# Scores of 64 queries on four quadrants, and longer tiled operations, in attention between two layers' matmuls

## The chip, the cores and the metric

The kernel runs on one core of a Trainium2 chip. Time is the device time of one execution in microseconds. TensorE does all matmuls and transposes, ScalarE, VectorE and GpSimd the elementwise work; SyncE and, for the first loads, GpSimd issue the DMAs.

## What is computed

Attention over 4 batches, 8 heads, 576 positions of 64 elements, then two feed-forward layers on its 2304 x 512 output. From the reference, shortened:

```
scores = where(causal, -1e9, q @ k.T / 8)                 # 576 x 576 of each head
a = exp(scores - max);  a /= a.sum + 1e-9;  local = a @ v
q_p = phi(q);  mem_out = (q_p @ M_prev) / (q_p . z_prev + 1e-6)
x = g * mem_out + (1 - g) * local                         # 2304 tokens x 512
h = x @ w_in;  r = max(h, 0);  x = (s * r * r + b) @ w_out         # first layer, 512 -> 2048 -> 512
h = x @ w2_in; g = piecewise quadratic of h;  out = g @ w2_out     # second layer
```

## The kernel before

**Units of work.** A head pair (hp) is two heads side by side on 128 partitions, 64 each. The queries of a batch are cut into tiles of 128 (t = 0 to 3) and a last one of 64 (t = 4). A part of attention is one batch and one of two groups: "lo" has tiles 1 and 0 (256 queries), "hi" has tiles 4, 3 and 2 (320 queries). The eight parts, the eight blocks of the first layer and the column sums stand in the program in an order of their own (ORDER); a part has four head pairs, so there are 16 head pairs of each group.

**One head pair.** att_load brings q and k (qk, two buffers) and q, M and v (nv, two buffers). att_front makes phi(q) over its norm and turns it (L796). att_scores writes the scores into PSUM banks ab (four, L826): with 64 elements to contract, each head uses one half of the array's rows, 64x128, and for the 64 queries of tile 4 a quadrant, 64x64, head 0 the first and head 1 the last. VectorE adds the mask and takes the minimum (L837), ScalarE the exponential (L522), and one of three engines scales the rows by the inverse of their sum (L861 to L863) in the arrays aa (four). att_flip turns 128x128 blocks of aa (L881) and copies them into at, au or av. att_sum accumulates the product with M (L896, whole array) and with v (L905, half of the columns for each head) in one bank, and writes the result's rounded and remaining part to xx. All of attention's matmuls are in plain fp32, which takes two records in the trace for each; transposes take one.

**The layers** work in rounded parts (three matmuls of 256 columns for each product: L951 to L953 and L1014, L1015, L1019 in the first layer; L1181 to L1237 and L1213 to L1255 in the second). The last block of the first layer is 512 wide. Their weights are in SBUF; the second layer's replace the first's as the last block is done with them, and its buffers lie where attention's were, so they open when attention has ended.

**What sets the order.** Every operation is given to a planner (Plan) with its engines, cost, dependencies and the slots of pools that it takes. The planner writes one order for each engine; then the program is emitted in it. A scores operation, a flip, a sum are each one entry on TensorE's queue, and nothing stands between their matmuls. While attention runs, layer-1 matmuls of an earlier block fill TensorE's queue between its operations. L1309 are matmuls on zeros that fill waits near the start. The planner gives a group of tiled matmuls the cost c_pair: 0.2 us, 1.667 ns a column and 4 ns a matmul.

Names in the trace: ab the four banks of attention, hb and yb the banks of the layers, wir and wor buffers that the first two parts borrow from weights.

Of the kernel before, what the change touches and what calls it, by code (L numbers as in the profile page):

```python
# [109 lines left out]
class Plan:  # L110
# [26 lines left out]
    def add(self, ways, r=(), w=(), pr=2, acq=()):  # L137
        i = len(self.ops)
        pre = set()
        slots = set(acq)  # L140
        for k in list(r) + list(w):
            s = k[0] if isinstance(k, tuple) else k
            if isinstance(s, Slot):
                slots.add(s)
# [225 lines left out]
def c_pair(n, k=1):  # L370

    return 0.2 + n * 1.667e-3 + k * 0.004
# [3 lines left out]
def tile_kernel(ctx: ExitStack, tc: tile.TileContext, qk_in, nv_in, z_prev, beta,  # L376
# [47 lines left out]
    zr = t32r([P, P], "zr")  # L424
    con = t32([P, 36], "con")
    cs_t = t32([P, NK], "cs")
# [138 lines left out]
    def constants():  # L565
# [6 lines left out]
        for j in range(2):  # L572
            dve(0.08, lambda rows=slice(64 * j, 64 * j + 64), j=j: nc.vector.tensor_scalar(
                con[rows, 32:36], con[rows, 16:24].rearrange("p (n two) -> p n two", two=2)[:, :, j], 1.0, None, ALU.mult), ["con"], ["con"], ATT)
        dma(lambda: con[:, 0:1], lambda: s_in.unsqueeze(0).broadcast_to([P, 1]), 512, w=["sb"], pr=W1)
        dma(lambda: con[:, 1:2], lambda: b_in.unsqueeze(0).broadcast_to([P, 1]), 512, w=["sb"], pr=W1)
# [224 lines left out]

    def att_scores(hp, g, qk, group):

        zs = [R_AB.take() for _ in range(1 + max(x for *_, places in group for x, _ in places))]
        new = []
        for t, c0, c1, _ in group:
            if t == 0:
                att_open[0] = (att_open[1][0], R_SM.take(), 256)  # L810
                new.append(att_open[0][1])
            elif c0 == 0:


                att_open[t] = ([(E_AA if early_part[0] else R_AA).take() for _ in range(1 if t == 4 else 2)], R_SM.take(), 0)
                new += att_open[t][0] + [att_open[t][1]]
# [12 lines left out]
        for t, c0, c1, places in group:  # L829
            w = t * P + rows_of(t)  # L830
            arrays, s, ao = att_open[t]
            nh = len(arrays)
# [3 lines left out]
            for j, (a, (x, at)) in enumerate(zip(arrays, places)):  # L836
                dve(c_dve(c1 - c0) + 0.02, alone(lambda a=a, s=s, z=zs[x], c0=c0, c1=c1, m0=m0, pi=pi, j=j, at=at, ao=ao: nc.vector.tensor_tensor_reduce(  # L837
                    a.t[:, ao + c0:ao + c1], z.t[:, at:at + c1 - c0], mask[:, m0:m0 + c1 - c0], -SCALE,
                    BIG if pi == 0 else s.t[:, j:j + 1], ALU.add, ALU.min, s.t[:, 2 * pi + j:2 * pi + j + 1])),
                    [zs[x], "mask", "zero_aa", (a, "new"), (s, "new")], [(a, t), (s, "min", j)], ATT)  # L840
            if c1 < w:
                continue
            for j, a in enumerate(arrays):
                def view(w=w, a=a, ao=ao):
                    return a.t[:, ao:ao + w]

                act(view, view, AF.Exp, w, [(s, "min", j)], [(a, t), (s, "sum", j)],
                    ATT, ap=2, bias=lambda s=s, x=2 * pi + j: s.t[:, x:x + 1], scale=-1.0,
                    accum_out=lambda s=s, x=4 + j: s.t[:, x:x + 1])
            c = 32 + hp if t == 4 else 16 + 2 * hp  # L850
            dve(0.13, lambda s=s, nh=nh, c=c: nc.vector.scalar_tensor_tensor(
# [3 lines left out]
            for j, a in enumerate(arrays):  # L855
# [3 lines left out]
                def col(s=s, j=j):  # L859
# [3 lines left out]
                     ("ACT", c_act(w, 1), lambda view=view, col=col: nc.scalar.activation(view(), view(), AF.Copy, scale=col()))],  # L863
                    [(s, "i")], [(a, t)], ATT)
        return [t for t, c0, c1, _ in group if c1 == t * P + rows_of(t)]

    def att_flip(t):

        nb = t + 1
        arrays, _, ao = att_open[t]  # L870
        at = R_AT[t].take()
# [3 lines left out]
        for c0, c1 in zip(cuts, cuts[1:]):  # L875
# [6 lines left out]
            pe((c1 - c0) * c_tr(P), flip, [(a, t) for a, kt in blocks[c0:c1] if kt == 0 or t == 4] + ["ident", "zero_aa"], [z, (at, "new", c0)],  # L882
               ATT, [z] + [at] * (c0 == 0))
# [3 lines left out]

    def att_sum(hp, b, g, nv, pg, ats):

        nq = GLEN[g]  # L890
        base = BASE[PARTS.index((b, g))]
        z = R_AB.take()
        keys = [x for t in GROUPS[g] for x in ats[t][1]]

        def go():
            nc.tensor.matmul(z.t[:, 0:nq], nv.t[:, NV_M[g]], pg.t[:, 0:nq], start=True, stop=False)  # L896
            off = 0
            for t in GROUPS[g]:
                n, nb, at = rows_of(t), t + 1, ats[t][0]
                for kt in range(nb):  # L900
                    for j in range(2):
                        last = t == GROUPS[g][-1] and kt == nb - 1
                        own = slice(64 * j, 64 * j + 64)
                        c = kt * P + j * n if t == 4 else (j * nb + kt) * P
                        nc.tensor.matmul(z.t[own, off:off + n], nv.t[:, NV_V[g] + kt, own], at.t[:, c:c + n],  # L905
                                         start=False, stop=last)
                off += n
        cols = nq + sum((t + 1) * rows_of(t) for t in GROUPS[g])
        pe(c_pair(cols, 12), go, [(nv, ""), pg] + keys, [z], ATT, [z])
        cuts = [0] + [c for c in range(nq) if c and (base + c) % XC == 0] + [nq]  # L910
        for a, e in zip(cuts, cuts[1:]):
            c = (base + a) % XC
            xk = x_keys(hp, c, c + e - a)
            rnd(lambda a=a, e=e, c=c: xh[hp][:, c:c + e - a], lambda a=a, e=e: z.t[:, a:e], e - a, [z], ["h" + x for x in xk], ATT, True)
            sub(lambda a=a, e=e, c=c: xl[hp][:, c:c + e - a], lambda a=a, e=e: z.t[:, a:e], lambda a=a, e=e, c=c: xh[hp][:, c:c + e - a],
                e - a, [z] + ["h" + x for x in xk], ["l" + x for x in xk] + [f"early{base}_{hp}"] * early_part[0], ATT, True)

    SCORES = {"lo": [[(1, 0, 256, ((0, 0), (1, 0))), (0, 0, 128, ((0, 256), (1, 256)))]],
              "hi": [[(4, 0, 512, ((0, 0),)), (4, 512, 576, ((1, 384),)), (2, 0, 384, ((1, 0), (2, 0)))],
                     [(3, 0, 512, ((0, 0), (1, 0)))]]}  # L920
    att_open = {}

    def att(i):
# [5 lines left out]
        first = True  # L929
        for hp in range(NP):  # L930
            qk, nv = att_load(b, hp, g, zb)
            if first:
                if "con" not in plan.lw:
                    constants()
                dma(lambda: zb.t, lambda: z_prev[b].rearrange("h d -> (h d)").unsqueeze(0).broadcast_to([P, H * D]),
                    P * H * D * 4, [], [zb], ATT if i == 0 else LOAD, [zb])
                first = False
            pg = att_front(hp, g, nv, zb)
            ats = {}
            for group in SCORES[g]:  # L940
                for t in att_scores(hp, g, qk, group):
                    ats[t] = att_flip(t)
            att_sum(hp, b, g, nv, pg, ats)
        plan.phase = None
# [432 lines left out]
```

## Time and profile before

| | |
|---|---|
| median of 3 runs | 1003.35 us (1003.24 to 1005.19) |
| the profiled execution | 1006.14 us |
| its span, first to last instruction | 1004.4 us |
| TensorE, VectorE, ScalarE, GpSimd busy | 992.5, 660.0, 589.0, 206.3 us |
| mean granted TensorE clock | 0.995 of full speed |

Busy time of an engine is the time in which at least one of its instructions is in flight; a matmul's duration holds its way through the array, so that neighbours overlap, and what one costs in a row is the distance of its start to the next one's.

### The profile page before, as it was taken

Reading aid. Unit: us, or ns where it says so; the run is one execution under the profiler, and the core shown is the slowest. Engines: PE = TensorE matmul, PEld = TensorE weight load, DVE = VectorE, ACT = ScalarE, POOL = GpSimd, SP = SyncE. Lnnn points to the kernel's source line nnn. Section 1 sums busy time; section 2 is a strip of 40 time slices with the busy share of each in tenths; the row PEclk is TensorE's granted clock in tenths of the full one; section 3 lists DMA queues with packets and bytes.
Section 4 is the critical chain, followed back from the end, with each engine's and each line's share of the span. In section 5 each row is a group of like instructions: output and inputs, shape, how many; then the busy total and the mean of one; then the engine's idle time right before and its main releaser. Section 6 shows DMA issues by size and latency. Waiting matters only on the chain.

```text
span 1004.4 us, 19651 instructions
## 1 busy us (share of the span) xinstructions
PE 992.5 (99%) x7480; PEld 878.5 (87%) x7480; DVE 660.0 (66%) x1545; ACT 589.0 (59%) x1331; POOL 206.3 (21%) x320
## 2 busy tenths in 40 slices
PE   8999999999999999999999999999999999999998
PEld 7799998898898889789898888999899998999987
DVE  5899855635644545554687885788769555576742
ACT  5999876646656655565556555666546434254323
POOL 5411133211110211111132321232234101011100
PEclk8999999999999999999999999999999999999999
DMA  9491034211221211211043334634354971231301
GB/s 321 170 410 60 15 92 140 70 52 49 76 70 48 85 62 56 68 60 46 1 152 132 127 116 143 225 126 147 110 185 162 355 248 46 82 95 32 106 27 37
DMA packets 50718, 115.57 MB, mean 115 GB/s; under 512 B 5440, under 2 KB 16192, under 8 KB 50624
## 3 DMA queue, kind: packets, MB, share of 16 engines
q1 hardware_dynamic: 50400, 113.73, 33.2%
q8 instruction: 59, 0.97, 0.4%
q0 software_dynamic: 224, 0.59, 0.3%
q14 instruction: 35, 0.29, 0.1%
HBM read 87.56 MB, written 26.74 MB: 114 GB/s over the span
## 4 chain that ended last, share of the span: by engine, by line
PE 91%; ACT 3%; DVE 2%; DMA 2%; issue 1%; SPq 0%; POOL 0%; DVEq 0%; POOLq 0%; ACTq 0%
PE hb L951 6%; PE hb L953 6%; PE hb L952 6%; PE ab L826 6%; PE yb L1014 5%; PE yb L1019 5%; PE yb L1015 5%; PE ab L905 4%; PE ab L881 4%; PE yb L1213 3%; PE yb L1214 3%; PE yb L1220 3%; PE ab L1220 3%; PE ab L1213 3%; PE ab L1214 3%; PE ab L1182 3%
## 5 line engine op out<-in xcount | busy, mean ns | idle before, releaser
L951 PE MATMUL hb<-xx,wi 128*128 128x256 f32 (+1 forms) x512 | 152.7, 298 | 0.0
L952 PE MATMUL hb<-xx,wi 128*128 128x256 f32 (+1 forms) x512 | 149.5, 292 | 0.0
L953 PE MATMUL hb<-xx,wi 128*128 128x256 f32 (+1 forms) x512 | 149.5, 292 | 0.0
L1014 PE MATMUL yb<-gg,wo 128*128 128x256 f32 (+1 forms) x394 | 102.6, 292 | 1.5 <-ACT gg L537 1.2
L951 PEld LDWEIGHTS hb<-xx,wi 128*128 128x128 f32 x512 | 96.4, 188 | 7.0 <-issue 3.5
L952 PEld LDWEIGHTS hb<-xx,wi 128*128 128x128 f32 x512 | 96.3, 188 | 2.8
L953 PEld LDWEIGHTS hb<-xx,wi 128*128 128x128 f32 x512 | 96.2, 188 | 2.9
L1015 PE MATMUL yb<-gg,wo 128*128 128x256 f32 (+1 forms) x394 | 98.0, 281 | 0.0
L522 ACT ACTIVATE aa<-aa,sm 128x384 f32<-128x384 f32 (+4 forms) x112 | 69.4, 621 | 48.2 <-DVE sm L837 48.0
L529 DVE TENSOR_TENSOR gg<-rr,gg 128x256 fp32r<-128x256 f32 (+1 forms) x102 | 44.6, 439 | 74.6 <-ACT gg L537 56.1
L1014 PEld LDWEIGHTS yb<-gg,wo 128*128 128x128 f32 x394 | 74.1, 188 | 9.0 <-issue 3.6
L837 DVE CUSTOM_DVE_ANT_0 aa<-ab,mask 128x512 f32<-128x512 f32 (+3 forms) x112 | 59.1, 553 | 32.9 <-PE ab L826 32.7
L995 ACT ACTIVATE rr<-hb 128x256 f32<-128x256 f32 (+1 forms) x105 | 42.8, 408 | 55.8 <-PE hb L953 52.8
L1015 PEld LDWEIGHTS yb<-gg,wo 128*128 128x128 f32 x394 | 74.2, 188 | 0.5
L1019 PE MATMUL yb<-gg,wo 128*128 128x256 f32 (+1 forms) x394 | 69.3, 288 | 0.0
L826 PE MATMUL ab<-qk 64*64 64x512 f32 (+5 forms) x320 | 58.4, 472 | 0.0
L1019 PEld LDWEIGHTS yb<-gg,wo 128*128 128x128 f32 x394 | 54.5, 188 | 2.4 <-issue 1.8
L861 POOL TENSOR_SCALAR aa<-aa,sm 128x384 f32<-128x384 f32 (+4 forms) x41 | 25.3, 619 | 149.1 <-DVE sm L854 114.8
L1182 PE MATMUL ab<-xx,wi 128*128 128x256 f32 x196 | 55.2, 282 | 0.0
L1181 PE MATMUL ab<-xx,wi 128*128 128x256 f32 x196 | 55.1, 281 | 0.0
L1183 PE MATMUL ab<-xx,wi 128*128 128x256 f32 x196 | 55.1, 281 | 0.0
L1181 PE MATMUL hb<-xx,wi 128*128 128x256 f32 x188 | 52.8, 281 | 0.0
(337 smaller groups left out, 2843.1 us busy)
## 6 DMA issues: line engine op xcount, KB each, us to landing
w2d<-st SPq DMA_DIRECT2D x48, 256.0 KB, 4.1
nv<-in_nv_dram SPq DMA_DIRECT2D x16, 576.0 KB, 3.7
wir<-in_moe_w_in_dram SPq DMA_DIRECT2D x16, 512.0 KB, 10.2
wor<-in_moe_w_out_dram SPq DMA_DIRECT2D x16, 512.0 KB, 10.2
raw<-in_moe_w_in_dram SPq DMA_DIRECT2D x16, 512.0 KB, 3.9
raw<-in_moe_w_out_dram SPq DMA_DIRECT2D x16, 512.0 KB, 4.4
qk<-in_qk_dram SPq DMA_DIRECT2D x16, 448.0 KB, 3.3
wo<-w2d SPq DMA_DIRECT2D x12, 512.0 KB, 5.1
```

The costliest lines, as they stand in the source:

```text
L522: nc.scalar.activation(o(), i(), func, **{a: b() if callable(b) else b for a, b in kw.items()})
L826: nc.tensor.matmul(zs[x].t[own if t == 4 else slice(0, n), at:at + c1 - c0], qk.t[own, q0:q0 + n], qk.t[own, k0 + c0:k0 + c1], start=True, ...
L951: nc.tensor.matmul(o, w_in_part(fi, 0)[:, kt, :], x_h(kt), start=kt == 0, stop=False)
L952: nc.tensor.matmul(o, w_in_part(fi, 0)[:, kt, :], x_l(kt), start=False, stop=False)
L953: nc.tensor.matmul(o, w_in_part(fi, 1)[:, kt, :], x_h(kt), start=False, stop=kt == NK - 1)
L1014: nc.tensor.matmul(yv(c), w_out_part(fi, 0)[:, cs], gg.t[0], start=fi == 0 and c % k == 0, stop=False)
L1015: nc.tensor.matmul(yv(c), w_out_part(fi, 1)[:, cs], gg.t[0], start=False, stop=False)
L1019: pe(c_mm(n), lambda c=c, cs=cs, gg=gg, fi=fi: nc.tensor.matmul(yv(c), w_out_part(fi, 0)[:, cs], gg.t[1], start=False, stop=fi == NF - 1 a ...
L1181: nc.tensor.matmul(o, sw(q, k, 0, kt), xo(k, 0, kt), start=j == 0 and kt == 0, stop=False)
L1182: nc.tensor.matmul(o, sw(q, k, 0, kt), xo(k, 1, kt), start=False, stop=False)
L1213: nc.tensor.matmul(y.t, gh.t[:, cs], wo2(q, i, 0), start=first and jj == 0, stop=False)
L1214: nc.tensor.matmul(y.t, gh.t[:, cs], wo2(q, i, 1), start=False, stop=False)
```

## The change

In tile 4 of an odd head pair the two heads' quadrants are exchanged (`turned`: head 0 writes the second half of the partitions), and att_scores takes items of two head pairs: the scores of tile 4 of both are one operation, on four quadrants. Tiles 2 and 3 of a head pair become one operation, where before tile 4 and 2 were one and tile 3 another. From the fourth 256-query part on (i > EARLY, which is 2) the head pairs of a part are taken two by two; for a 256-query part the scores of both are one operation, and so are both products with v. The first three parts keep their form (`lo1`). A `dict` in place of a `set` fixes the order in which slots are looked at.

```diff
-        slots = set(acq)
+        slots = dict.fromkeys(acq)
...
+    def turned(hp, t):
+        return int(t == 4 and hp % 2)
...
-    def att_scores(hp, g, qk, group):
+    def att_scores(g, items):
...
-            for t, c0, c1, places in group:
+            for hp, qk, t, c0, c1, places in items:
...
-                    nc.tensor.matmul(zs[x].t[own if t == 4 else slice(0, n), at:at + c1 - c0], qk.t[own, q0:q0 + n],
+                    o = 64 * (j ^ turned(hp, t))
+                    nc.tensor.matmul(zs[x].t[slice(o, o + 64) if t == 4 else slice(0, n), at:at + c1 - c0], qk.t[own, q0:q0 + n],
                                      qk.t[own, k0 + c0:k0 + c1], start=True, stop=True)
-        pe(c_pair(sum(c1 - c0 for _, c0, c1, _ in group), len(group)), scores, [(qk, "")], zs + [(x, "new") for x in new], ATT, zs + new)
+        cols = sum(c1 - c0 for _, _, t, c0, c1, _ in items) - sum(c1 - c0 for hp, _, t, c0, c1, _ in items if turned(hp, t))
+        pe(c_pair(cols, len(items)), scores, [(qk, "") for qk in dict.fromkeys(x[1] for x in items)], zs + [(x, "new") for x in new], ATT, zs + new)
...
-    def att_sum(hp, b, g, nv, pg, ats):
+    def att_sum(hps, b, g, nvs, pgs, ats):
...
+            for x, hp in enumerate(hps):
+                nc.tensor.matmul(z.t[:, x * nq:x * nq + nq], nvs[hp].t[:, NV_M[g]], pgs[hp].t[:, 0:nq], start=x == 0, stop=False)
...
-    SCORES = {"lo": [[(1, 0, 256, ((0, 0), (1, 0))), (0, 0, 128, ((0, 256), (1, 256)))]],
-              "hi": [[(4, 0, 512, ((0, 0),)), (4, 512, 576, ((1, 384),)), (2, 0, 384, ((1, 0), (2, 0)))],
-                     [(3, 0, 512, ((0, 0), (1, 0)))]]}
+    SCORES = {"lo1": [[(0, 1, 0, 256, ((0, 0), (1, 0))), (0, 0, 0, 128, ((0, 256), (1, 256)))]],
+              "lo": [[(0, 1, 0, 256, ((0, 0), (1, 0))), (0, 0, 0, 128, ((0, 256), (1, 256))),
+                      (1, 1, 0, 256, ((2, 0), (3, 0))), (1, 0, 0, 128, ((2, 256), (3, 256)))]],
+              "hi": [[(0, 4, 0, 512, ((0, 0),)), (1, 4, 0, 512, ((1, 0),)), (0, 4, 512, 576, ((2, 0),)), (1, 4, 512, 576, ((3, 0),))],
+                     [(0, 2, 0, 384, ((0, 0), (1, 0))), (0, 3, 0, 512, ((2, 0), (3, 0)))],
+                     [(1, 2, 0, 384, ((0, 0), (1, 0))), (1, 3, 0, 512, ((2, 0), (3, 0)))]]}
...
+        k = 1 if i <= EARLY else 2
+        for h0 in range(0, NP, k):
+            hps = range(h0, h0 + k)
...
+            for group in SCORES[g if k > 1 else "lo1"]:
+                for hp, t in att_scores(g, [(h0 + x, qks[h0 + x], t, c0, c1, places) for x, t, c0, c1, places in group]):
+                    ats[hp][t] = att_flip(hp, t)
+                    done = len(ats[hp]) == len(GROUPS[g])
+                    if done and (g == "hi" or hp == hps[-1]):
+                        att_sum([hp] if g == "hi" else list(hps), b, g, nvs, pgs, ats)
```

On TensorE, in the first part with 320 queries, the second head pair's tiles 4 and 2 stood in a row like this before, with its tile 3 some thirty rows further on (ab_113 to ab_116 are the four banks, qk_159 and qk_160 the two buffers of q and k; a row's last figures are partitions x columns of the result):

```order
L1019 MATMUL yb_111<-gg,wo_930 128x256
L826 MATMUL ab_116<-qk_160 64x512 x2
L826 MATMUL ab_115<-qk_160 64x64 x2
L826 MATMUL ab_115<-qk_160 128x384
L826 MATMUL ab_114<-qk_160 128x384
L896 MATMUL ab_113<-pt_170,nv_161 128x320
```

After the change the same part's queue has tile 4 of both head pairs by itself, and tiles 2 and 3 of the first some fifty rows later (L833 is what L826 was, L972 to L974 are L951 to L953, L1035 and L1036 are L1014 and L1015):

```order
L974 MATMUL hb_109<-xx,wi_1148 128x256
L833 MATMUL ab_116<-qk_159 64x512 x2
L833 MATMUL ab_114<-qk_160 64x512 x2
L833 MATMUL ab_115<-qk_159 64x64 x2
L833 MATMUL ab_113<-qk_160 64x64 x2
L972 MATMUL hb_109<-xx,wi_1148 128x256
...
L1036 MATMUL yb_112<-gg,wo_1203 128x256
L833 MATMUL ab_115<-qk_159 128x384
L833 MATMUL ab_113<-qk_159 128x384
L833 MATMUL ab_114<-qk_159 128x512
L833 MATMUL ab_116<-qk_159 128x512
L1035 MATMUL yb_112<-gg,wo_1203 128x256
```

The change from quadrants to row halves inside an operation is gone, and each of the new operations writes all four banks. The second place is the products with v in the fourth 256-query part, on TensorE too; before, those of a head pair stood alone (pt holds the turned phi(q), at and av the turned weights of the values):

```order
L953 MATMUL hb_109<-xx,wi_778 128x256
L896 MATMUL ab_116<-pt_170,nv_161 128x256
L905 MATMUL ab_116<-at_184,nv_161 64x128 x4
L905 MATMUL ab_116<-av_187,nv_161 64x128 x2
L881 MATMUL ab_115<-ident,aa_174 128x128 x2
```

Now two head pairs' products stand together in one bank (L905 is what L896 was, L915 what L905 was):

```order
L1036 MATMUL yb_111<-gg,wo_907 128x256
L905 MATMUL ab_116<-pt_170,nv_161 128x256
L905 MATMUL ab_116<-pt_171,nv_162 128x256
L915 MATMUL ab_116<-at_184,nv_161 64x128 x4
L915 MATMUL ab_116<-av_187,nv_161 64x128 x2
L915 MATMUL ab_116<-at_185,nv_162 64x128 x4
L915 MATMUL ab_116<-av_188,nv_162 64x128 x2
L1035 MATMUL yb_112<-gg,wo_907 128x256
```

One step to half arrays and one back serve what needed two of each.

## Rows read from the trace of the kernel before

**Rows 1.** The page's busy time of each engine (us, share, instructions).

```profile
PE 992.5 (99%) x7480; PEld 878.5 (87%) x7480; DVE 660.0 (66%) x1545; ACT 589.0 (59%) x1331; POOL 206.3 (21%) x320
```

**Rows 2.** Busy time by stage: from:to, length, engines (instructions), clock, DMA share, GB/s.

```profile
0.00:120.00 120.00, 114.09 (x930) 104.39 (x931) 103.01 (x301) 107.80 (x291) 35.53 (x73) 0.97 0.54 201
120.00:505.00 385.00, 385.00 (x3546) 333.69 (x3545) 206.08 (x669) 234.37 (x610) 64.04 (x117) 1.00 0.21 65
505.00:1004.40 499.40, 493.38 (x3008) 440.41 (x3007) 350.93 (x578) 246.88 (x430) 106.73 (x130) 1.00 0.39 133
```

**Rows 3.** What TensorE waited for (us in total, times, longest).

```profile
PE ab L826 <- DMA wir<-in_qk_dram: 3.2, 2, 1.7
PE yb L1014 <- ACT gg L537: 1.2, 1, 1.2
```

**Rows 4.** TensorE's timeline at tile 3's scores: start, us, line, count.

```profile
441.19 0.62 PE L1019 MATMUL yb<-gg,wo 128*128 128x256 f32 x4
441.75 1.13 PE L826 MATMUL ab<-qk 64*128 64x512 f32 x4
442.81 0.39 PE L951 MATMUL hb<-xx,wi 128*128 128x256 f32 x1
443.03 0.28 PE L952 MATMUL hb<-xx,wi 128*128 128x256 f32 x1
443.15 0.28 PE L953 MATMUL hb<-xx,wi 128*128 128x256 f32 x1
```

**Rows 5.** The same at scores of 256 and 128 columns in one operation.

```profile
160.17 0.92 PE L826 MATMUL ab<-qk 64*128 64x256 f32 x8
161.03 0.38 PE L951 MATMUL hb<-xx,wi 128*128 128x256 f32 x1
```

**Rows 6.** The same at tiles 4 and 2 and the products behind them.

```profile
481.45 2.04 PE L826 MATMUL ab<-qk 64*64 64x512 f32 x12
483.41 0.81 PE L896 MATMUL ab<-pt,nv 128*128 128x320 f32 x2
484.15 0.80 PE L905 MATMUL ab<-at,nv 128*64 128x64 f32 x20
484.78 1.04 PE L905 MATMUL ab<-au,nv 128*64 128x128 f32 x16
485.66 0.82 PE L905 MATMUL ab<-av,nv 128*64 128x128 f32 x12
486.41 0.62 PE L1019 MATMUL yb<-gg,wo 128*128 128x256 f32 x3
```

**Rows 7.** The same behind tile 3's scores of that head pair: transposes.

```profile
475.56 0.38 PE L1014 MATMUL yb<-gg,wo 128*128 128x256 f32 x1
...
476.14 0.82 PE L881 MATMUL ab<-ident,aa 128*128 128x128 f32 x6
476.72 0.37 PE L1014 MATMUL yb<-gg,wo 128*128 128x256 f32 x1
476.92 0.28 PE L1015 MATMUL yb<-gg,wo 128*128 128x256 f32 x1
...
479.66 1.03 PE L881 MATMUL ab<-ident,aa 128*128 128x128 f32 x8
480.45 0.36 PE L1014 MATMUL yb<-gg,wo 128*128 128x256 f32 x1
```

**Rows 8.** DMA issues: KB each, median us from issue to landing.

```profile
qk<-in_qk_dram SPq DMA_DIRECT2D x16, 448.0 KB, 3.3
```

**Rows 9.** Groups by form, 481.4 to 483.45 us: busy us, mean ns.

```profile
L826 PE MATMUL ab<-qk 64*64 64x512 f32 x4 | 1.1, 614 | 0.0
```

**Rows 10.** Busy time between attention and layer 2, whose first matmul is L1235.

```profile
503.00:529.30 26.30, 25.08 (x217) 24.76 (x216) 22.99 (x43) 15.01 (x36) 9.30 (x6) 1.00 0.45 156
529.30:618.30 89.00, 89.00 (x398) 72.54 (x397) 64.63 (x123) 49.91 (x92) 20.80 (x34) 1.00 0.35 120
...
L1235 PE MATMUL ab<-xp,wi x24: 281/281/283, 618.3 to 993.8; 128*128 128x256 f32 x24
```

More of the change, by code (lines that the diff above doesn't have):

```diff
@@ L143, in add @@
             if isinstance(s, Slot):
-                slots.add(s)
+                slots[s] = None
         for k in r:
@@ L424, in tile_kernel @@
     zr = t32r([P, P], "zr")
-    con = t32([P, 36], "con")
+    con = t32([P, 40], "con")
     cs_t = t32([P, NK], "cs")
@@ L574, in constants @@
                 con[rows, 32:36], con[rows, 16:24].rearrange("p (n two) -> p n two", two=2)[:, :, j], 1.0, None, ALU.mult), ["con"], ["con"], ATT)
+            dve(0.08, lambda rows=slice(64 * j, 64 * j + 64), j=j: nc.vector.tensor_scalar(
+                con[rows, 36:40], con[rows, 16:24].rearrange("p (n two) -> p n two", two=2)[:, :, 1 - j], 1.0, None, ALU.mult), ["con"], ["con"], ATT)
         dma(lambda: con[:, 0:1], lambda: s_in.unsqueeze(0).broadcast_to([P, 1]), 512, w=["sb"], pr=W1)
@@ L863, in att_scores, with att_flip @@
                      ("ACT", c_act(w, 1), lambda view=view, col=col: nc.scalar.activation(view(), view(), AF.Copy, scale=col()))],
-                    [(s, "i")], [(a, t)], ATT)
-        return [t for t, c0, c1, _ in group if c1 == t * P + rows_of(t)]
-    def att_flip(t):
+                    [(s, "i")], [(a, hp, t)], ATT)
+        return [(hp, t) for hp, _, t, c0, c1, _ in items if c1 == t * P + rows_of(t)]
+    def att_flip(hp, t):
         nb = t + 1
-        arrays, _, ao = att_open[t]
+        arrays, _, ao = att_open[hp, t]
         at = R_AT[t].take()
@@ L881, in flip @@
                     nc.tensor.transpose(z.t[:, x * P:x * P + P], a.t[:, ao + kt * P:ao + kt * P + P], ident)
-            pe((c1 - c0) * c_tr(P), flip, [(a, t) for a, kt in blocks[c0:c1] if kt == 0 or t == 4] + ["ident", "zero_aa"], [z, (at, "new", c0)],
+            pe((c1 - c0) * c_tr(P), flip, [(a, hp, t) for a, kt in blocks[c0:c1] if kt == 0 or t == 4] + ["ident", "zero_aa"], [z, (at, "new", c0)],
                ATT, [z] + [at] * (c0 == 0))
@@ L892, in att_sum @@
         z = R_AB.take()
-        keys = [x for t in GROUPS[g] for x in ats[t][1]]
+        keys = [x for hp in hps for t in GROUPS[g] for x in ats[hp][t][1]]
         def go():
[L896 to L907, printed above, removed]
@@ L918, in tile_kernel @@
-    SCORES = {"lo": [[(1, 0, 256, ((0, 0), (1, 0))), (0, 0, 128, ((0, 256), (1, 256)))]],
-              "hi": [[(4, 0, 512, ((0, 0),)), (4, 512, 576, ((1, 384),)), (2, 0, 384, ((1, 0), (2, 0)))],
-                     [(3, 0, 512, ((0, 0), (1, 0)))]]}
+            for x, hp in enumerate(hps):
+                nc.tensor.matmul(z.t[:, x * nq:x * nq + nq], nvs[hp].t[:, NV_M[g]], pgs[hp].t[:, 0:nq], start=x == 0, stop=False)
+            for x, hp in enumerate(hps):
+                off = x * nq
+                for t in GROUPS[g]:
+                    n, nb, at = rows_of(t), t + 1, ats[hp][t][0]
+                    for kt in range(nb):
+                        for j in range(2):
+                            last = hp == hps[-1] and t == GROUPS[g][-1] and kt == nb - 1
+                            own = slice(64 * j, 64 * j + 64)
+                            c = kt * P + (j ^ turned(hp, t)) * n if t == 4 else (j * nb + kt) * P
+                            nc.tensor.matmul(z.t[own, off:off + n], nvs[hp].t[:, NV_V[g] + kt, own], at.t[:, c:c + n],
+                                             start=False, stop=last)
+                    off += n
@@ new lines, in att_sum @@
+        cols = len(hps) * (nq + sum((t + 1) * rows_of(t) for t in GROUPS[g]))
+        pe(c_pair(cols, 12), go, [(nvs[hp], "") for hp in hps] + [pgs[hp] for hp in hps] + keys, [z], ATT, [z])
+        cuts = [0] + [c for c in range(nq) if c and (base + c) % XC == 0] + [nq]
+        for x, hp in enumerate(hps):
+            for a, e in zip(cuts, cuts[1:]):
+                c = (base + a) % XC
+                xk = x_keys(hp, c, c + e - a)
+                rnd(lambda a=a, e=e, c=c, hp=hp: xh[hp][:, c:c + e - a], lambda a=a + x * nq, e=e + x * nq: z.t[:, a:e], e - a, [z], ["h" + x for x in xk], ATT, True)
+                sub(lambda a=a, e=e, c=c, hp=hp: xl[hp][:, c:c + e - a], lambda a=a + x * nq, e=e + x * nq: z.t[:, a:e],
+                    lambda a=a, e=e, c=c, hp=hp: xh[hp][:, c:c + e - a],
+                    e - a, [z] + ["h" + x for x in xk], ["l" + x for x in xk] + [f"early{base}_{hp}"] * early_part[0], ATT, True)
@@ L929, in att @@
         first = True
[L930 to L943, printed above, removed]
+        k = 1 if i <= EARLY else 2
+        for h0 in range(0, NP, k):
+            hps = range(h0, h0 + k)
+            qks, nvs, pgs, ats = {}, {}, {}, {hp: {} for hp in hps}
+            for hp in hps:
+                qks[hp], nvs[hp] = att_load(b, hp, g, zb)
+                if first:
+                    if "con" not in plan.lw:
+                        constants()
+                    dma(lambda: zb.t, lambda: z_prev[b].rearrange("h d -> (h d)").unsqueeze(0).broadcast_to([P, H * D]),
+                        P * H * D * 4, [], [zb], ATT if i == 0 else LOAD, [zb])
+                    first = False
+            for hp in hps:
+                pgs[hp] = att_front(hp, g, nvs[hp], zb)
+            for group in SCORES[g if k > 1 else "lo1"]:
[4 more added lines that the diff above has]
+                        att_sum([hp] if g == "hi" else list(hps), b, g, nvs, pgs, ats)
         plan.phase = None
```

30 lines of the change are left out of this document (11 added, 19 removed).

## The prediction

> **What bounds the kernel now.** I read the page's busy times first, then the busy time by stage, then what TensorE waited for, then single stretches of its timeline. TensorE is busy 992.5 of 1004.4 us [rows 1]. By stage [rows 2]: in the 385 us from 120 to 505, where all sixteen head pairs with 320 queries run between layer-1 matmuls, it is busy 385.00 us, while VectorE (206) and ScalarE (234) have room. Its waits lie at the start (3.2 us for the first loads) and one of 1.2 us in layer 1 [rows 3]. So in the stage that the change edits the end moves by what TensorE's own work loses, unless a new wait appears.
>
> A busy TensorE is not one that computes without loss. The prices of a tiled operation come from starts in the timeline, since the durations overlap. A layer-1 matmul of 256 columns starts 0.11 us after the one before it. Four of them ahead of the scores of 128 queries should take 441.19 to 441.65; the scores start at 441.75, so **entry** costs 0.10. The scores of 512 key columns then take 1.06 us to the next start (441.75 to 442.81), and the first layer-1 matmul behind them takes 0.22, so **return** costs 0.11 [rows 4]. Scores of 384 columns took 0.86 (160.17 to 161.03) [rows 5]; the difference is 1.56 ns per column. Values' products of 512 columns inside one operation took 0.88 (484.78 to 485.66), 1.72 ns [rows 6]. I take 1.64 per column, two quadrants or half arrays at a time, and so **0.22 fixed** within an operation of scores (1.06 less 0.84). The operation with the last 64 queries, 576 columns on two quadrants and then 384 on two row halves, took 1.96 (481.45 to 483.41) [rows 6]: less 960 columns (1.57) and 0.22 there are **0.17 for the change of shape** in its middle. The values' product took 2.26 (484.15 to 486.41) for 1216 columns (1.99): 0.27 fixed.
>
> **The change, part by part.** *Quadrants.* The 16 head pairs with 64 last queries have 576 columns each, on two quadrants. Two pairs now use all four: 8 x 576 columns x 1.64 ns = 7.6 us less (7.2 to 7.9 by the two column prices).
> *Fewer stretches.* I counted in the order of both kernels how often TensorE goes from whole-array work to tiled work: 78 times before, 66 after. 12 x (0.10 + 0.11) = 2.5 us. Runs of 64x128 scores fall from 46 to 28: 18 x 0.22 = 4.0. The 16 changes of shape go: 16 x 0.17 = 2.7; but eight operations on quadrants now stand by themselves, and their fixed part is in no row: between the 0.17 of a quadrant run that goes on to row halves and the 0.22 of a 64x128 run; I take 0.20, 1.6 back (1.4 to 1.8). The two joined values' products of the fourth 256-query part save 2 x 0.27 = 0.5.
> *More returns from transposes.* Stretches of transposes that go straight to layer 1 rise from 77 to 92. The first layer-1 matmul behind one takes 0.20 instead of 0.11; but six transposes took 0.58 and eight 0.79 [rows 7], 0.105 for each one added, so that a stretch is about 0.05 shorter than its count: 15 x 0.04 = 0.6 back (0 to 1.4).
> Sum: 7.6 + 2.5 + 4.0 + 2.7 - 1.6 + 0.5 - 0.6 = **15.1 us** of TensorE time (13.7 to 16.2 by these bounds). Both kernels have the same matmuls otherwise.
> *The rest* (four more columns of con, filled by two short VectorE operations near the start, and longer names of dependencies) cost nothing as long as TensorE's first loads are what it waits for there [rows 3]. No row has their form; VectorE's mean over the first 120 us is 103.01 / 301 = 0.34 us an operation [rows 2], and two of that size uncovered would be 0.7, which the range holds.
> *Waits that are added.* A scores operation now takes all four ab banks, and one of 64x128 runs also all four aa arrays, so a second head pair's scores can't be issued while the first pair's are read. What is queued behind a waiting scores matmul or transpose is all of layer 1, on the same engine. Before, a scores operation of 512 columns ended at 475.56 and its transposes started at 479.66, 4.1 us later, without a wait [rows 7]. In the changed order the shortest work between a scores operation and its own first transposes is, by these prices, 4.1 us too (4.6 behind quadrants). Both qk buffers belong to one pair of pairs, so the second is loaded again between its last scores and the next quadrant operation: at the closest place 47 layer-1 matmuls and 6 transposes stand there, 47 x 0.11 + 6 x 0.105 = 5.8 us and the fixed parts, against 3.3 us from issue to landing [rows 8]. SyncE's queue holds an nv load and the stores of x2d behind that load, and none of these is due within microseconds. I put 1.2 us for new waits, one more of the size of the one in layer 1 [rows 3]; the bounds are 0 and, if half of the 24 new scores operations wait 0.3 us, 3.6.
> The profiled execution took 1006.14, 1.7 more than its span: 1006.14 - 15.1 + 1.2 = 992.2. It was 2.8 above the median of the runs shown, 1003.35, from which the same sum gives **989.5 us**. About 0.2% is what a measurement of this kernel can tell from no change.
>
> **A rule against the change.** In the operation before, the two quadrants of one head pair write one ab bank, from different row halves of the array. The window of that operation has four records of 64x512 with a mean of 614 ns in 1.1 us of busy time [rows 9]: two ran at a time. The Trainium skill (TensorEngine Tiling, "Gotcha 1: PSUM Pressure") says that different row tiles cannot access the same PSUM bank at the same time; by that the new operation, which has both row halves in each of two banks, could not run four at a time. The row disagrees for two quadrants, and no run here shows four. By the rule the quadrants' 7.6 us would not come, and the sum would be 997.
>
> **The rivals.**
> *Two at a time.* Four moving streams may not overlap, for whatever reason: nothing in the trace has more than two at once, two row halves [rows 4], two column halves [rows 6], or two opposite quadrants [rows 9]. Each pairing that the four need has a precedent there: same rows with other columns, same columns with other rows, opposite corners. Then only the fixed parts are saved, 7.5 us, with the waits 997.
> *Less cover for the second layer's weights.* In the changed order 69 layer-1 matmuls (7.9 us) stand between the last values' product and the first 512-wide matmul of layer 1's last block; before there are 207 (23.6 us), and it took from 503.0 to 529.3. In that time column sums run on VectorE (busy 23.0 of 26.3) and the second layer's first weights land; then the last block and the rest of the weights, VectorE 64.6 of 89.0 us, to the first matmul of layer 2 at 618.3 [rows 10]. VectorE's 87.6 us must now fit in some 99. They do, with 12 to spare; should the weights' chain be exposed by the whole 15.7 us, nothing of the change is left (1005); exposed by half, 997.
> *Bank waits, slower than before.* All four banks in one operation make the chain scores, four reductions, exponentials, scaling, transposes, copies run one pair at a time; TensorE takes its queue in order, so a late copy stops layer 1. It decides at 15.1 / 24 = 0.63 us per operation; at 0.75 each the time is 1006. For it: the last copies and the next scores stand about 1 us apart in the order. Against it: the same was so before (transposes end at 480.45, scores start at 481.45 [rows 6, 7]), and the stage had no wait at all.
> *No change*: quadrants don't overlap, and the waits take the rest.
>
> **How the numbers follow.** The forecast (986 to 993) 0.70; two at a time (995 to 999) 0.10; less cover (992 to 1003) 0.12; slower 0.05; no change 0.03. Likeliest 989.5. Low end: no new waits, the one of 1.2 us gone as well and the sum at 16.2, which gives 986. High end 998: with two at a time and most of less cover inside, some 0.12 are left out. Faster by over 0.2% (under 1001.3): 0.70 + 0.10 + 0.11 = 0.91; within 0.2%: 0.04; slower 0.05.
>
> **What would show it.** Right: four 64x512 starts within some 20 ns and a quadrant operation of about 1.2 us from start to the next one's start; scores of 896 columns in 1.7; TensorE busy about 15 us less, and still without idle time between 120 us and the last values' product. Wrong: quadrant operations of 2.1 us; idle time ahead of scores or transposes put down to a copy on ScalarE or VectorE, or to a qk load; idle time between the end of attention and layer 2 put down to weights; a longer first 120 us, whose order shifts slightly and which the sum leaves unchanged.

## The result, and the profile after

The changed kernel takes 992.92 us (median of four runs, 992.27 to 994.67) against 1003.65 us (four runs, 1003.24 to 1005.19): a ratio of 0.989, interval 0.988 to 0.991, or 10.7 us less. In later comparisons the kernel before had medians between 1004.5 and 1005.4, and the changed one again 992.88, so that about 12 us is the better figure. The forecast was 989.5, its range 986 to 998. The profiled execution took 993.02 us with a span of 990.8; before, 1006.14 and 1004.4. The two profiled times differ by 13.1 us and their spans by 13.6, where the prediction had 13.9.

TensorE's busy time, from the page, and busy time by stage (columns as in [rows 2]):

```profile
PE 978.8 (99%) x7480; PEld 877.8 (89%) x7480; DVE 645.8 (65%) x1529; ACT 594.7 (60%) x1356; POOL 203.2 (21%) x314
```

```profile
0.00:120.00 120.00, 113.33 (x933) 103.50 (x934) 100.92 (x300) 106.62 (x289) 35.55 (x74) 0.97 0.53 201
120.00:492.00 372.00, 372.00 (x3519) 334.78 (x3518) 188.09 (x639) 232.05 (x612) 60.49 (x112) 1.00 0.21 67
492.00:990.80 498.80, 493.51 (x3033) 439.48 (x3029) 356.83 (x591) 255.99 (x456) 107.13 (x128) 1.00 0.40 133
```

TensorE has as many instructions as before [rows 1] and is busy 13.7 us less, and from 120 to 492 us it still has no idle time. In the first 120 us its busy time differs by 0.8 us [rows 2]. Its idle time is 12.0 us in all (span less busy time), before 11.9. So it is work that went, not a wait. What TensorE waited for:

```profile
PE ab L833 <- DMA wir<-in_qk_dram: 3.5, 1, 3.5
PE hb L1330 <- DVE zr L562: 1.1, 1, 1.1
PE ab L798 <- POOL wor L790: 0.8, 1, 0.8
PE yb L1035 <- ACT gg L537: 0.6, 1, 0.6
PE hb L972 <- ACT rr L1016: 0.4, 1, 0.4
```

The first three end at 12.35, 1.06 and 45.05 us, near the start like the loads in [rows 3], and the last two add up to 1.0 us. None is ahead of scores or transposes in the middle of attention: the new wait of 1.2 us that the sum allowed did not come.

The operation on four quadrants, first in TensorE's timeline (start, us, line, count), then in its groups by form:

```profile
184.79 0.28 PE L974 MATMUL hb<-xx,wi 128*128 128x256 f32 x1
185.00 1.20 PE L833 MATMUL ab<-qk 64*64 64x512 f32 x16
186.14 0.39 PE L972 MATMUL hb<-xx,wi 128*128 128x256 f32 x1
186.36 0.28 PE L973 MATMUL hb<-xx,wi 128*128 128x256 f32 x1
```

```profile
L833 PE MATMUL ab<-qk 64*64 64x512 f32 x8 | 1.1, 614 | 0.0
```

From its start to the next one's are 1.14 us; the forecast was about 1.2 for all four quadrants and 2.1 if two ran at a time. The group is read against [rows 9]: there four records of 614 ns in 1.1 us, here eight of 614 ns in the same 1.1 us. The first four records of the operation at 306.20 start within 20 ns. The Trainium skill's rule that different row tiles cannot use one PSUM bank at the same time (TensorEngine Tiling, "Gotcha 1: PSUM Pressure") is not what this trace shows: each of two banks took both row halves here, and all four ran together. The halves write different partitions of the bank, and none of these matmuls adds to what is there; other cases no run here shows.

Scores of tiles 2 and 3, 896 columns:

```profile
399.11 0.28 PE L974 MATMUL hb<-xx,wi 128*128 128x256 f32 x1
399.31 1.77 PE L833 MATMUL ab<-qk 64*128 64x384 f32 x8
401.02 0.39 PE L972 MATMUL hb<-xx,wi 128*128 128x256 f32 x1
```

1.71 us from start to start, forecast 1.7. Last, the stretch between attention and layer 2, which answers to [rows 10]:

```profile
508.00:516.00 8.00, 8.00 (x72) 7.99 (x71) 6.80 (x12) 3.03 (x8) 0.06 (x1) 1.00 0.76 263
516.00:606.10 90.10, 89.19 (x395) 71.75 (x394) 74.73 (x137) 59.46 (x115) 29.50 (x34) 1.00 0.42 138
```

From the first matmul behind the last values' product to the first of layer 2 it is 98.1 us (508.0 to 606.1), before 115.3 (503.0 to 618.3): 17.2 us shorter, where the prediction counted 15.7 and left VectorE some 99. VectorE is busy 81.5 us in it, and TensorE idles 0.9, less than the 1.2 before 529.3.

### The profile page after: what moved, and what is told of

Its sections match the earlier page's. It is cut to its first block, busy times and chain, and to the rows that moved or that the text cites. A ratio compares the mean times of both kernels' runs of the same rounds, so it can differ in the third digit from the quotient of the medians.

```text
span 990.8 us, 19659 instructions
## 1 busy us (share of the span) xinstructions
PE 978.8 (99%) x7480; PEld 877.8 (89%) x7480; DVE 645.8 (65%) x1529; ACT 594.7 (60%) x1356; POOL 203.2 (21%) x314
## 4 chain that ended last, share of the span: by engine, by line
PE 86%; ACT 7%; issue 2%; DMA 2%; DVE 1%; POOL 1%; SPq 0%; DVEq 0%; POOLq 0%; ACTq 0%
PE hb L972 5%; PE hb L974 5%; PE hb L973 5%; PE yb L1035 5%; PE ab L833 5%; PE yb L1040 5%; PE yb L1036 4%; PE ab L915 4%; PE ab L889 4%; PE ab L1234 3%; PE ab L1235 3%; PE ab L1241 3%; PE yb L1241 3%; PE yb L1235 3%; PE yb L1234 3%; PE ab L1202 3%
## 5 line engine op out<-in xcount | busy, mean ns | idle before, releaser
L972 PE MATMUL hb<-xx,wi 128*128 128x256 f32 (+1 forms) x512 | 154.4, 302 | 0.4 <-ACT rr L1016 0.4
L974 PE MATMUL hb<-xx,wi 128*128 128x256 f32 (+1 forms) x512 | 150.0, 293 | 0.0
L1035 PE MATMUL yb<-gg,wo 128*128 128x256 f32 (+1 forms) x394 | 105.8, 298 | 0.6 <-ACT gg L537 0.6
L972 PEld LDWEIGHTS hb<-xx,wi 128*128 128x128 f32 x512 | 96.3, 188 | 9.0 <-issue 4.9
L1036 PE MATMUL yb<-gg,wo 128*128 128x256 f32 (+1 forms) x394 | 99.4, 282 | 0.0
L974 PEld LDWEIGHTS hb<-xx,wi 128*128 128x128 f32 x512 | 96.7, 189 | 2.9
L522 ACT ACTIVATE aa<-aa,sm 128x384 f32<-128x384 f32 (+4 forms) x112 | 69.3, 621 | 32.0 <-DVE sm L845 32.0
L1035 PEld LDWEIGHTS yb<-gg,wo 128*128 128x128 f32 x394 | 74.2, 188 | 9.2 <-issue 6.3
L1036 PEld LDWEIGHTS yb<-gg,wo 128*128 128x128 f32 x394 | 74.3, 189 | 0.4
L845 DVE CUSTOM_DVE_ANT_0 aa<-ab,mask 128x512 f32<-128x512 f32 (+3 forms) x112 | 56.1, 553 | 20.2 <-PE ab L833 20.2
L1040 PE MATMUL yb<-gg,wo 128*128 128x256 f32 (+1 forms) x394 | 68.7, 287 | 0.0
L529 DVE TENSOR_TENSOR xx<-ab,xx 128x256 fp32r<-128x256 f32 (+3 forms) x36 | 14.7, 422 | 63.6 <-ACT xx L537 63.3
L1202 PE MATMUL hb<-xx,wi 128*128 128x256 f32 x188 | 52.8, 281 | 0.0
L1203 PE MATMUL hb<-xx,wi 128*128 128x256 f32 x188 | 52.8, 281 | 0.0
```

Source lines behind the costliest of these rows:

```text
L522: nc.scalar.activation(o(), i(), func, **{a: b() if callable(b) else b for a, b in kw.items()})
L972: nc.tensor.matmul(o, w_in_part(fi, 0)[:, kt, :], x_h(kt), start=kt == 0, stop=False)
L974: nc.tensor.matmul(o, w_in_part(fi, 1)[:, kt, :], x_h(kt), start=False, stop=kt == NK - 1)
L1035: nc.tensor.matmul(yv(c), w_out_part(fi, 0)[:, cs], gg.t[0], start=fi == 0 and c % k == 0, stop=False)
L1036: nc.tensor.matmul(yv(c), w_out_part(fi, 1)[:, cs], gg.t[0], start=False, stop=False)
L1040: pe(c_mm(n), lambda c=c, cs=cs, gg=gg, fi=fi: nc.tensor.matmul(yv(c), w_out_part(fi, 0)[:, cs], gg.t[1], start=False, stop=fi == NF - 1 a ...
```

## The experiments

**Two at a time.** The changed kernel's order, with tile 4 of both head pairs on the same two quadrants. The planner's cost keeps the old count, so that the order is the same.

```diff
     def turned(hp, t):
+        return 0
+
+    def counted(hp, t):
         return int(t == 4 and hp % 2)
...
-        cols = ... if turned(hp, t))
+        cols = ... if counted(hp, t))
```

> The changed kernel with the quadrants of odd head pairs not exchanged: both head pairs' last 64 queries use the same two quadrants, in the same order of all engines. Theory (four quadrants run at once and TensorE is the bound): each of the eight operations takes 0.96 us longer, 7.6 us in all, about 1000.5. Rival (the gain came from fewer steps to tiled work, and quadrants lie beside other work): 993 to 995.

Measured: 1001.11 us (1000.41 to 1002.15), ratio 0.996 (0.995 to 0.998), 8.2 us above the changed kernel. Its first such operation, in groups by form and in the timeline:

```profile
L836 PE MATMUL ab<-qk 64*64 64x512 f32 x8 | 1.9, 602 | 0.0
```

```profile
184.73 2.17 PE L836 MATMUL ab<-qk 64*64 64x512 f32 x16
186.82 0.39 PE L975 MATMUL hb<-xx,wi 128*128 128x256 f32 x1
```

The same eight records fill 1.9 us in place of 1.1, and the operation lasts 2.09 us in place of 1.14; eight of them are 7.6 us. In both traces TensorE's 7480 matmuls stand in one order. This is the term of the quadrants by itself, and most of the gain.

**Tiles 2 and 3 apart**, each an operation of its own; tile 4 stays on four quadrants.

```diff
-                     [(0, 2, 0, 384, ((0, 0), (1, 0))), (0, 3, 0, 512, ((2, 0), (3, 0)))],
-                     [(1, 2, 0, 384, ((0, 0), (1, 0))), (1, 3, 0, 512, ((2, 0), (3, 0)))]]}
+                     [(0, 2, 0, 384, ((0, 0), (1, 0)))], [(0, 3, 0, 512, ((0, 0), (1, 0)))],
+                     [(1, 2, 0, 384, ((0, 0), (1, 0)))], [(1, 3, 0, 512, ((0, 0), (1, 0)))]]}
```

> The changed kernel with the scores of tiles 2 and 3 of a head pair as two operations of two banks each; the four quadrants stay. Theory (each step to tiled work and back costs 0.21 and each run 0.22): 39 runs in place of 28 and 77 steps in place of 66 cost 11 x 0.43 = 4.7, less 18 returns from transposes x 0.04 = 0.7, so 997. Rival (operations that take all four banks make TensorE or its fillers wait): some of that comes back, 993 to 995.

Measured: 998.22 us (997.06 to 1000.89), ratio 0.994 (0.992 to 0.995), 5.3 us above the changed kernel. One new wait is in it:

```profile
PE hb L972 <- ACT rr L1016: 1.5, 1, 1.5
```

It is on layer 1's own activations, 1.1 us more than after. That leaves 4.2 us where the expectation had 4.0. But the order changed too: layer-1 matmuls of 256 columns start 115.5 ns apart on average, after 115.9 (last section), some 0.7 us over 1,706 of them, so that the runs and steps by themselves cost nearer to 4.9. Nothing came back from smaller demands on the banks, so this run too speaks against bank waits.

**Tile 3 first** within an operation of 896 columns; a test of what sets the rate of the layer's matmuls behind it (last section).

```diff
-            for hp, qk, t, c0, c1, places in items:
+            for hp, qk, t, c0, c1, places in sorted(items, key=lambda x: -(x[2] == 3)):
```

> The changed kernel with tile 3's scores issued ahead of tile 2's inside their operation, nothing else moved. In the changed kernel the layer-1 matmuls of 256 columns behind these operations start 118 ns apart, in the kernel before mostly 113. If what stands last in the operation decides that, they are 113 apart here and the time falls by up to 2 us; if not, the spacing stays and the time is the same, or longer by some tenths, since the reductions of tile 2 can start only 0.85 us later.

Measured: 992.72 us (991.9 to 993.73), ratio 0.988 (0.987 to 0.989), the time of the changed kernel, and the rate is the same. Which tile stands last doesn't set it.

**The 256-query parts pair by pair**, in all parts.

```diff
-        k = 1 if i <= EARLY else 2
+        k = 1 if g == "lo" else 2
```

> The changed kernel with the fourth 256-query part taken one head pair at a time as before; the 320-query parts keep the change. By the prices of the prediction: 3 more steps to tiled work x 0.21, 2 more runs of scores x 0.22 and 2 more products with v x 0.27 cost 1.6, about 994.5. Rival (joining makes pairs wait for each other): the same time or less than the changed kernel's.

Measured: 991.73 us (991.44 to 992.39), ratio 0.987 (0.986 to 0.989): 1.2 us below the changed kernel, where the prediction's prices made it slower. The whole order moves with this edit. In the trace behind 120 us, attention's operations take 0.8 us more with the pairs apart, the way that the prices say, but the layers' matmuls take 1.7 less: 256-column ones start 115.4 ns apart on average, after 115.9, which is 0.8 of it. What made the rest no run parts.

**A planner's price nearer to the trace**: the fixed part of tiled work, 0.10 + 0.22 + 0.11 us in [rows 4], stood in the planner as 0.2.

```diff
-    return 0.2 + n * 1.667e-3 + k * 0.004
+    return 0.4 + n * 1.667e-3 + k * 0.004
```

> The changed kernel with the planner's fixed cost of a tiled operation at 0.4 us instead of 0.2, near the 0.43 that the rows give (entry, fixed part, return). If the planner's wrong price leaves waits, the time falls by the 1 to 2 us that they hold; if TensorE's work alone decides, the time stays within 1 us of the changed kernel's 993.

Measured: 991.78 us (990.34 to 992.87), ratio 0.987 (0.986 to 0.989), about 1 us below the changed kernel. Two of its runs, at a mean granted clock of 0.996 and 0.997, took 992.7 and 992.9 us, as the changed kernel does; two at 0.998 and 1.000 took 990.8 and 990.3. So it is inside the scatter, and goes with the clock.

**Breaks in layer 2**, where no tiled work stands: ahead of the first product of sixteen blocks one 64x128 matmul of 32 columns.

```diff
+                if name == "P1" and j == 0:
+                    nc.tensor.matmul(z.t[:, 0:32], ident[0:64, :], ident[0:64, 0:32], start=True, stop=True)
```

> The changed kernel with one short tiled matmul (64 rows, 32 columns, overwritten by what follows) ahead of the first of every seven products of layer 2, 16 in all. In all traces so far the 256-column matmuls of layer 2 start 118 ns apart, those of layer 1 behind a tiled operation of up to 576 columns 113 apart, behind one of 896 columns 118. If a short break sets the closer spacing, the 84 matmuls of 256 columns behind each are 113 to 114 apart, 0.4 us less, against some 0.35 for the break: about the changed kernel's time, and a longer life of the spacing would show. If the spacing belongs to layer 2's operands, it stays 118 and the time grows by some 5 us.

Measured: 1000.03 us (999.18 to 1000.86), ratio 0.996 (0.994 to 0.997), 7.2 us above the changed kernel, 0.45 us a break. One of them in the timeline:

```profile
642.00 0.28 PE L1206 MATMUL hb<-xx,wi 128*128 128x256 f32 x1
642.21 0.40 PE L1202 MATMUL ab<-ident 64*128 64x32 f32 x2
642.54 0.39 PE L1204 MATMUL ab<-xx,wi 128*128 128x256 f32 x1
642.76 0.28 PE L1205 MATMUL ab<-xx,wi 128*128 128x256 f32 x1
```

0.21 into it where the layer's matmuls follow at 0.12, 0.33 in it for 0.05 of columns, 0.22 behind it: entry, fixed part and return come with the change of tile shape, with no attention near. By these starts a break costs 0.53 us more than the two layer matmuls alone (0.76 us from 642.00 to 642.76), 8.5 us for sixteen; some 1.1 come back from closer spacing behind it (last section). The expectation had 0.35 for a break, and either about no change or 5 us; both were too low.

**Both kernels again**, for the difference that the rest is read against.

> The kernel before, unchanged, timed and profiled once more, because its first profiled execution (1006.1 us) lay 2.5 above its median, while the changed kernel's (993.0) lay on its median. If that execution was a slow draw, a second profile has a span of 1001 to 1002.5 us and the difference to the first shows in which stage executions vary; if a profile of this kernel is always longer than its other executions, the span is 1004 again. Time 1003.5 either way.

> The changed kernel once more, beside these on one chip. From the two profiled spans (1004.4 and 990.8) and the sum of the prediction the difference to the kernel before is 12 to 14 us, more than the 10.7 of the first four runs of each: ratio 0.987 to 0.988. If the first runs were typical, 0.989.

Measured: 1004.95 us (eleven runs, 1003.97 to 1006.17), ratio 1.000 (0.999 to 1.001), and 992.88 us (992.58 to 993.66), ratio 0.988 (0.987 to 0.990). The four runs in the result were low ones of the kernel before, and the expectation of 1003.5 was 1.4 us too low. Its second profiled execution took 1006.17 us with a span of 1004.3, like the first (1006.14, 1004.4), so that both lie above its medians, and the difference of the profiles is larger than the one of the medians.

**The two small gains together**: the 256-query parts pair by pair, and the price of 0.4.

> The 256-query parts taken pair by pair throughout, and the planner's cost of a tiled run raised from 0.2 to 0.4 us; each alone came out about 1.1 us under the changed kernel. If the two gains are separate causes, they add: about 990.6 us. If both are the same thing (another order near the start, or layer-1 matmuls at the shorter spacing for more of the time), or chance of the order, they don't: 991 to 992.5 us. Against the kernel before (about 1004.7) a ratio of 0.986 or 0.987.

Measured: 989.98 us (989.24 to 992.56), ratio 0.985 (0.983 to 0.988), the fastest of all, 2.9 us below the changed kernel. Three of its four runs had a mean granted clock of 0.999 or 1.000 and took 989.2 to 990.1 us; the fourth had 0.996 and took 992.56. The changed kernel's runs had 0.995 to 0.997. So I read the start, with TensorE's busy time and granted clock (the last but two figures, as a share of 2.4 GHz) in 1 us slices, after:

```profile
9.00:10.00 1.00, 0.00 (x0) 1.00 0.78 280
10.00:11.00 1.00, 0.00 (x0) 1.00 0.92 361
11.00:12.00 1.00, 0.00 (x0) 0.79 1.02 398
12.00:13.00 1.00, 0.65 (x4) 0.50 0.96 369
...
17.00:18.00 1.00, 1.00 (x10) 0.50 0.98 380
18.00:19.00 1.00, 0.89 (x8) 0.80 1.02 395
```

and the first scores in the timeline of the changed kernel, then of this version:

```profile
12.35 3.30 PE L833 MATMUL ab<-wir 64*128 64x256 f32 x16 [3.48 <-DMA wir<-in_qk_dram]
```

```profile
11.08 1.58 PE L833 MATMUL ab<-wir 64*128 64x256 f32 x16 [1.81 <-DMA wir<-in_qk_dram]
```

In the 3.48 us of idle time the clock fell from 2.4 to 1.2 GHz (0.50), for some 6.8 us by the slices, and the same sixteen records took 3.30 us in place of 1.58. With 1.81 us of idle time it stayed up. In the kernel before it fell too, from 12 to 19 us, behind two waits of 1.67 and 1.56 us:

```profile
10.41 0.92 PE L826 MATMUL ab<-wir 64*128 64x256 f32 x8 [1.67 <-DMA wir<-in_qk_dram]
12.89 1.44 PE L826 MATMUL ab<-wir 64*128 64x256 f32 x6 [1.56 <-DMA wir<-in_qk_dram]
```

```profile
12.00:13.00 1.00, 0.10 (x2) 0.60 1.04 412
```

So the two profiles of the result both have such a stretch, and it doesn't make their difference. Two kernels tested what it is worth.

**Zeros ahead of the first scores**: twelve more matmuls on zeros into a bank that the scores then overwrite, in the changed kernel, and in the fastest version.

```diff
         def scores():
+            for _ in range(12 if first else 0):
+                nc.tensor.matmul(zs[0].t[:, 0:P], f(zr), f(zr), start=True, stop=True)
```

> The changed kernel with twelve matmuls on zeros (24 records, about 2.2 us at the rate of those ahead of them) put ahead of its first scores, where TensorE sat idle for 3.48 us, after which the granted clock was 0.50 of full speed from 12 to 18 us. Theory: that idle time is what lets the clock fall, and the half-speed stretch is worth some 2 us of the whole time and most of its scatter. Then the clock stays at 1.00 from 10 to 20 us and the time is 990 to 991 us, with a mean granted clock of 0.999 or 1.000 in most runs. Rival: the start is bound by loads, and the clock there costs nothing; then 992.5 to 993.5 us, with or without the fall.

> The same twelve matmuls in the version with the 256-query parts pair by pair and a planner's price of 0.4 us. By the theory its gain over the changed kernel was mostly the clock at the start, which held in three of its four runs: then it is now at 989 to 990 us, no more than 1 us under the changed kernel with the zeros. If its order is worth the whole 2.9 us by itself, it is 988 or less, 2 to 3 us under that kernel.

Measured: 992.14 us (991.66 to 992.7), ratio 0.987 (0.985 to 0.988), and 991.24 us (990.37 to 991.81), ratio 0.986 (0.984 to 0.987). The changed kernel with the zeros:

```profile
9.33 2.84 PE L831 MATMUL ab<-zr 128*128 128x128 f32 x24
12.67 0.92 PE L840 MATMUL ab<-wir 64*128 64x256 f32 x8 [0.50 <-DMA wir<-in_qk_dram]
13.86 0.92 PE L840 MATMUL ab<-wir 64*128 64x256 f32 x8 [0.26 <-DMA wir<-in_qk_dram]
```

The clock stayed at 1.00 from 10 to 20 us, and all eight runs of the two had 0.999 or 1.000: that the idle time lets it fall holds. The worth of it was put too high: the changed kernel gains 0.8 us, not two. The traces say the same: without counting the zeros, the work behind the first 60 records starts 0.82 us earlier, that behind the first 4000 records 0.87. Its first q and k land late either way (12.67 us against 12.35), and a wait of 0.26 us stands among the first sixteen records, so that the scores behind them start only 0.69 us earlier (15.62 against 16.31). The fastest version stands 1.3 us higher with the zeros. In the profiled execution without them its clock was up already; with them the work behind the first 4000 records starts 0.3 us later, and from 534 us on it is 0.9 later. Between the two kernels with zeros, at one clock, 0.9 us remain for the order; the clock and the order together make the 2.9, in shares that these runs, each some tenths wide, don't part further.

## Why the prediction was right

**What bounds the kernel.** TensorE's own work in attention did bound it: 13.7 us less busy time, 13.6 us less span.

**Quadrants**, 7.6 us: 8.2 when they were undone, 7.6 from the operations' own lengths (2.09 less 1.14, eight times). Here a row of two at a time was extended to four on the ground that each pairing had a precedent; that step carried the forecast, and it held.

**Scores as a whole.** In the 320-query parts a head pair's scores took 1.97 and 1.06 us, 48.4 for sixteen; now eight operations of 1.13 and sixteen of 1.70 take 36.3. That is 12.1 us less, and the terms for the quadrants, for sixteen runs and for the changes of shape give 7.6 + 3.5 + 2.7 - 1.6 = 12.2.

**Fewer runs and steps.** Splitting tiles 2 and 3 again (11 runs and 11 steps more, less the returns from transposes) cost 5.3 us with 1.1 of a wait, so 4.2, where these prices gave 4.0. The traces have the steps and runs as counted: 78 and 46 before, 66 and 28 after.

**Where two errors cancel.** I added the times from each matmul's start to the next one's by kind of operation, in both traces (us):

| | before | after | difference |
|---|---|---|---|
| scores | 65.8 | 52.4 | -13.4 |
| transposes | 49.7 | 46.7 | -3.0 |
| products with M and with v | 69.3 | 67.5 | -1.8 |
| matmuls on zeros | 19.2 | 20.7 | +1.5 |
| both layers and sums of columns | 794.7 | 797.7 | +3.0 |

These times hold TensorE's idle time too, and an entry falls to what stands ahead of a tiled operation, a return to what stands behind it. Without the idle time the differences are -12.0, -3.2, -1.7, -0.5 and +3.9. Scores lost 12.0 where the sum's terms for them (7.6 + 4.0 + 2.7 - 1.6) gave 12.7. Steps, joined products and returns from transposes lie in the transposes, the products and the layers; the sum had 2.5 + 0.5 - 0.6 = 2.4 us for them. The returns move between these rows: 13 products with M stood directly behind scores and paid the return (0.74 us against 0.63 for 320 columns), and 2 do now, while 9 more layer-1 matmuls do. What the sum put at nothing is that layer-1 matmuls of 256 columns start further apart, 2.2 us in all (last section); the prediction had "the same matmuls otherwise". Without these 2.2 the three rows lost 3.3. So scores lost 0.7 less than the sum had, the steps and returns 0.9 more, the zeros another 0.5, the slower matmuls took 2.2 back, and 1.2 us for new waits was not needed. The errors have opposite signs: the sum less the waits, 13.9, is right to 0.3 us of the 13.6 between the spans partly by luck.

**The joined part.** The joining of the fourth 256-query part should gain 1.6 us by the terms for steps and joined products, and the kernel without it is 1.2 us faster. The two traces show the saving in attention's operations (0.8 us) and the loss in the layers' matmuls (1.7), of which the spacing, which was not in the sum, is 0.8.

**The last step, from span to median**, made 1.1 to 2.0 of the 3.4 us between forecast and result. I took the sum from the median of three runs, 1003.35; from the later medians of 1004.5 to 1005.4 the same sum gives 990.6 to 991.5. The rest has two parts. At a mean granted clock of 0.995 to 0.997 the median spans are 1003.6 us before (28 runs of the later comparisons) and 990.75 after (all 8), 12.9 apart and not 13.9. And 12 of 51 later runs of the kernel before kept the clock at 0.999 or 1.000 and were shorter, 1001.7 to 1002.7, while none of the changed kernel's did.

**The rivals.** Two at a time: the trace and its experiment speak against it. Less cover for layer 2's weights: the cover did shrink, by 1.5 us more than counted, and TensorE lost nothing by it, since VectorE's work fitted in the shorter stretch. Bank waits: TensorE has no idle time between 120 and 492 us. No change: the time fell by 1.1%.

## What to carry to other kernels

Price tiled matmuls as entry, fixed part, columns and return, each from two starts in the timeline; on a saturated TensorE fewer and fuller stretches were worth nearly what that count said here, 13.6 us of busy time against 15.1. Two heads of 64 elements with 64 queries each fill half of the array; four such products on the four quadrants cost the time of two. Before a difference of 2 us is put down to the order, look at the granted clock of each run, and at idle time ahead of the first loads.

## What the runs showed of the hardware that was not expected

**Two rates of the same matmul.** Layer-1 matmuls of 256 columns run at one of two spacings, and which one goes with the tiled work ahead of them. After, behind a quadrant operation, and behind an operation of 896 columns (groups of lines in the two stretches, from 389.7 to 394.6 us and from 401.25 to 405.4 us; mean ns of one is the last figure but one):

```profile
L973 PE MATMUL hb<-xx,wi 128*128 128x256 f32 x10 | 2.8, 276 | 0.0
L1036 PE MATMUL yb<-gg,wo 128*128 128x256 f32 x5 | 1.2, 276 | 0.0
```

```profile
L973 PE MATMUL hb<-xx,wi 128*128 128x256 f32 x8 | 2.2, 280 | 0.0
L1036 PE MATMUL yb<-gg,wo 128*128 128x256 f32 x4 | 1.0, 281 | 0.0
```

In the first there are 44 steps from the start at 389.69 us to the one at 394.68, 113.4 ns each; in the second 36 from 401.24 to 405.48, 117.8 ns each, at a granted clock of 1.00 in both. It is no chance: between 120 and 500 us before, all 16 stretches behind scores are at the faster rate; after, all 8 behind quadrants are, and 15 of the 16 behind 896 columns are at the slower one, the same in the repeated run. With the tiles apart, 10 of the 12 behind 384 columns alone are fast, and 1 of the 3 where 512 columns follow directly on 384. All of layer 2 after, with no tiled work, is slow, at 117.8 ns. Behind each break there the spacing falls within some eight steps to 113.4 and stays there until the next matmuls of 512 columns, for 82 steps at the longest; behind those it is 117.8 again in all places but one. So the operation of 896 columns, which saves its fixed part, gives some of it back in the layer behind it: over 120 to 500 us the mean spacing rises from 114.6 to 115.9 ns over some 1,750 matmuls, 2.2 us in all.

Neither the last tile (the run with tile 3 first) nor the length alone decides. Four of the 16 stretches before stand directly behind tiles 4 and 2, 960 columns in 1.97 us, longer than the 896 columns in 1.70, and all four are fast; one of them from 468.86 to 473.75 us, 43 steps of 113.7 ns:

```profile
466.67 2.04 PE L826 MATMUL ab<-qk 64*64 64x512 f32 x12
468.64 0.39 PE L1014 MATMUL yb<-gg,wo 128*128 128x256 f32 x1
468.86 0.28 PE L1015 MATMUL yb<-gg,wo 128*128 128x256 f32 x1
```

Behind the two operations of 768 columns after, one stretch is slow and one fast. By what mechanism the rate is set, no run here shows.

**Four quadrants at once**: four streams on 64x64 quadrants start within 20 ns of each other and take no longer than two (eight records in 1.1 us, four on two quadrants in 1.1), with both row halves in one bank, on different partitions of it.

**The clock at the start**: 3.48 us of idle time behind the zeros brought 1.2 GHz for some 6.8 us, and so did two waits of 1.67 and 1.56 us with 0.92 us of scores between them; one of 1.81 us, with scores behind it, did not. It accounts for part of the scatter: in the comparison with the fastest version the kernel before had spans of 1002.2 to 1002.4 us in runs with a mean clock of 0.999 or 1.000, and 1003.6 to 1004.7 at 0.996 or 0.997.
